# Stores of an intermediate result moved from the ScalarE queue to SP, other stores merged and put off, in a fused FFT filter and two MoE layers on one Trainium2 core

## The chip, the core and the metric

The kernel runs on one core of a Trainium2 chip. That core has a matrix engine (TensorE, "PE"; its weight loads are shown apart as "PEld"), a vector engine (VectorE, "DVE"), ScalarE ("ACT"), GpSimd ("POOL") and SyncE ("SP"), which here does nothing but issue DMAs, in order. ACT and POOL can issue DMAs too. The metric is device time in microseconds; before the change it is 1584.96 us, the median of three runs from 1580.27 to 1590.88 us.

## What is computed

```python
X = np.fft.rfft(x, axis=1)                      # x: 8 x 3072 x 256
Yr = Xr @ w_r - Xi @ w_i + b_r
Yi = Xr @ w_i + Xi @ w_r + b_i
Yr, Yi = softshrink(Yr, 0.01), softshrink(Yi, 0.01)
a = np.fft.irfft(Yr + 1j * Yi, n=3072, axis=1)  # 24576 tokens of 256

h = np.maximum(a @ w_in, 0)                     # 256 -> 2048
y = (s * h * h + b) @ w_out                     # 2048 -> 256

logits = y @ w_gate                             # 8 experts, top 1, 768 places each
out[i] = gate[i] * (relu(y[i] @ w1[e]) @ w2[e]) # only for tokens that got a place
```

Places are given in the order of the tokens, so most of the 24576 tokens get none and their output row is zero.

## The kernel before, in words

**The Fourier filter.** A batch of 3072 rows is transformed in two steps. The first (`f1_mm`, L224) multiplies chunks of x by a 48-point matrix; eight chunks make a batch, and each chunk's result `z` goes to the DRAM tensor `zd`. The second takes the batch in twelve groups, p = 0 to 11, each two frequency rows wide: `g_load` (L264) brings `zp` back from `zd`, `g_a` makes the spectrum (`pf`, `l`), `g_b` and `g_b2` mix it with the weights (`pmx`, `kb`, `t`), `g_soft` shrinks it (`cl`, `t`), `g_c` (L388) does the first step back (`pi`) and copies it to `v`, which goes to the DRAM tensor `vd`. The last step back (`i2_load` L400, `i2_mm` L407, `i2_rows` L428) reads `u` from `vd`, eight pieces i to a batch, writes the transposed activations `ah` on ACT and, for later, `at` with two DVE transposes; `at` goes to the DRAM tensor `ad`.

**The first MoE layer as logits.** For each piece the kernel runs eight units (`s_unit`, L748): four matmuls `ph`, a Relu `r` on ACT and a square `qb` on DVE. A batch is thus 64 units, numbered 0 to 63. Only bounds of the logits are needed for most tokens. Four exact blocks of 256 tokens are computed in full in batch 1 (`x_steps`, L1000: `phx`, `xq`, and a store of `xq` to `sd`), and the few candidates for a place at the end.

**What sets the order.** `run` (L1763) writes the program out by unit: it emits `s_unit`, then the put-off stores in the list `later`, then what the table `plan` holds for this unit, sorted by rank. The plan is made by `plan_batch`: the groups of batch b run during batch b - 1, one group each five units, with steps at the offsets of `GROUP_STEPS` (`g_a` 0, `g_b` 2, `g_b2` 4, `g_soft` 4.1, `g_c` 8) from a start that lies `GROUP_LEAD` = 9 units before that batch's unit 0. A group's `zp` load is emitted six units ahead of its `g_a` (four for p = 0 and 1). `i2_do`, the chunks of the first step and the logits go to the unit in a small window where the sum of planned work is lowest (`best`, L1898). The groups of batch 1 run in batch 0, on a tighter cycle. Within a unit each engine runs in program order.

**DMAs.** All DMAs issued by SP and ACT share eight completion semaphores, shown as DMAHW0 to DMAHW7 in the orders below. They are given out in turn over both engines, and a DMA waits until the last DMA on its semaphore has landed. Before the change `v` is stored by ACT right after its copy (L395, L397); a `z` chunk is stored by SP with four DMAs (L246) one unit after its copy; `at` likewise with four; an `xq` store is emitted right behind its square (L1021). The tiles behind these stores rotate: `v` and `zp` have three buffers, `z` and `xq` share two.

Of the kernel before, what the change touches and what calls it, by code (L numbers as in the profile page):

```python
# [19 lines left out]
C = 256  # L20
# [3 lines left out]
M1 = 48  # L24
# [7 lines left out]
TD = 256  # L32
# [92 lines left out]
S_FROM, S_TO = 19, 62  # L125
LIST_AT = 60
XP = 3
INV_LOAD_AT = 54
FIRST_GROUPS_AT = 26
GROUP_LEAD = 9  # L130
GROUP_CYCLE = 5
GROUP_STEPS = (("g_a", 0), ("g_b", 2), ("g_b2", 4), ("g_soft", 4.1), ("g_c", 8))
FIRST_STEPS = (("g_a", 0.3), ("g_b", 1.3), ("g_b2", 2), ("g_soft", 2.6), ("g_c", 5))
# [17 lines left out]
class Kern:  # L151
# [54 lines left out]
    def f1_load(self, b, c):  # L206

        xv = self.I["x"][b].rearrange("(a n) c -> a n c", n=M2)
        if b == 0 and c % 2 == 1:
            xs = [self.stage()[:, 0:2 * C].rearrange("p (n c) -> p n c", n=2) for k in range(2)]  # L210
            for k in range(2):
                for r in range(2):
                    n2 = 8 * c + 4 * r + 2 * k
                    self.nc.sync.dma_start(out=xs[k][64 * r:64 * r + M1], in_=xv[:, n2:n2 + 2, :])
        else:
            pool, tag = (self.mo, "u") if b == 0 and c > 3 else (self.wk, "x")
            xp = pool.tile([128, 4, C], F32, tag=tag, name="x", bufs=4 if tag == "x" else 3)
            for r in range(2):
                n2 = 8 * c + 4 * r
                self.nc.sync.dma_start(out=xp[64 * r:64 * r + M1], in_=xv[:, n2:n2 + 4, :])  # L220
            xs = [xp[:, 0:2], xp[:, 2:4]]
        self.xt[b, c] = xs

    def f1_mm(self, b, c):  # L224

        nc = self.nc
        xs = self.xt.pop((b, c))
        if b or c % 2 == 1:
            ph = self.hp.tile([128, 2, 512], F32, tag="h", name="pz")
            ps = [ph[:, 0], ph[:, 1]]  # L230
        else:
            ps = [self.psum("pz") for r in range(2)]
        for k in range(2):
            for r in range(2):
                h = slice(64 * r, 64 * r + M1)
                nc.tensor.matmul(ps[r][64 * k:64 * k + 64, :], self.f1[h], xs[k][h].rearrange("p a c -> p (a c)"),  # L236
                                 start=True, stop=True, skip_group_check=True)
        if b:
            zz = self.wk.tile([128, 2, 2, C], F32, tag="z", name="z", bufs=2)
            nc.scalar.copy(out=zz.rearrange("p r a c -> p r (a c)"), in_=ph)  # L240

            def store():
                for r in range(2):
                    for k in range(2):
                        n2 = 8 * c + 4 * r + 2 * k
                        nc.sync.dma_start(out=self.zs[b][n2:n2 + 2].rearrange("n q c -> q n c"), in_=zz[64 * k:64 * k + M1, r])  # L246
            self.later.append(store)
            return
        for r in range(2):
            t = 2 * c + r  # L250
            k = t % 11
            pool, tag, n = ((self.wk, "v", 3), (self.wk, "t", 3), (self.mo, "ah", 2), (self.mo, "asq", 2),
                            (self.wk, "zp", 3))[min(k // 2, 4)]
            z = pool.tile([128, 2, C], F32, tag=tag, name="z", bufs=n)
            if r == 1:
                nc.vector.tensor_copy(out=z.rearrange("p a c -> p (a c)"), in_=ps[r])
            else:
                nc.scalar.copy(out=z.rearrange("p a c -> p (a c)"), in_=ps[r])
            for k in range(2):
                n2 = 8 * c + 4 * r + 2 * k  # L260
                nc.sync.dma_start(out=self.zs[b][n2:n2 + 2].rearrange("n q c -> q n c"), in_=z[64 * k:64 * k + M1])
# [126 lines left out]
    def g_c(self, b, p):  # L388
        nc = self.nc
        t = self.Y.pop((b, p))  # L390
        ps = self.psum("pi1")
        for gi in range(2):
            nc.tensor.matmul(ps[:, gi * C:(gi + 1) * C], self.e[:, 2 * p + gi], t[:, gi * C:(gi + 1) * C], start=True, stop=True)  # L393
        v = self.wk.tile([128, 512], F32, tag="v", name="v", bufs=3)
        nc.scalar.copy(out=v, in_=ps)  # L395
        dst = self.vd[b].rearrange("n (r g) c -> (n r) (g c)", r=4)
        nc.scalar.dma_start(out=dst[:, 2 * p * C:(2 * p + 2) * C], in_=v)  # L397


    def i2_load(self, b, i):  # L400
# [49 lines left out]
    def f1_items(self, b):  # L450
        it = []
        for k in range(8):
            def f(k=k):
                self.f1_mm(b, k)
                if b:
                    self.x_ahead(8 * b + k + (XP if b < 3 else XP - 1))
            it.append(f)
        return it

    def x_ahead(self, n):  # L460

        while self.xn <= min(n, 8 * self.B - 1):
            self.f1_load(*divmod(self.xn, 8))
            self.xn += 1
# [535 lines left out]
    def x_steps(self, dtile, lgpool, ga, out, m0, hidden, rows, ptile, keep=None, yout=None):  # L1000

        nc = self.nc
        x = {}
        qs, ys = {}, {}

        def a():
            x["a"] = self.x_in(dtile(), ga(), ptile)
            x["lg"] = lgpool()
            if yout is not None:
                x["y"] = ptile("ya").rearrange("p (m c) -> p m c", m=2)  # L1010

        def mm(v):
            ps = hidden()
            self.x_mm(ps, x["a"], v)
            q = qs[v] = rows()
            nc.scalar.activation(out=q, in_=ps, func=AF.Relu)
            nc.vector.tensor_tensor(out=q, in0=q, in1=q, op=ALU.mult)
            if yout is not None:
                ys[v] = self.x_out(x["y"], q, v)
            if keep is not None:  # L1020
                nc.sync.dma_start(out=keep[2 * v:2 * v + 2, :, 128 * m0:128 * m0 + TD].rearrange("f p n -> p f n"), in_=q)  # L1021

        def lg(v):
            for k in (v, v + 1):
                self.x_lg(x["lg"], qs, k)
            if yout is not None:
                for k in (v, v + 1):
                    ys.pop(k)()

        def end():  # L1030
            ls = self.rp.tile([128, TD], F32, tag="ls", name="ls2", bufs=1)
            nc.scalar.copy(out=ls, in_=x["lg"][:, :TD])
            x["ls"] = ls
            if yout is not None:
                y = self.pb.tile([128, 2, C], F32, tag="y", name="y", bufs=1)
                nc.vector.scalar_tensor_tensor(out=y, in0=x["y"], scalar=self.ws, in1=self.yb.unsqueeze(1).to_broadcast([128, 2, C]),
                                               op0=ALU.mult, op1=ALU.add)
                nc.sync.dma_start(out=yout.rearrange("(m p) c -> p m c", p=128), in_=y)

        def fin():  # L1040
            pt = ptile("plt")
            for m in range(2):
                nc.tensor.transpose(pt[:, m * 128:(m + 1) * 128], x["ls"][:, m * 128:(m + 1) * 128], self.ident)
            nc.vector.tensor_reduce(
                out=out[:, m0:m0 + 2], in_=pt[:, :TD].rearrange("p (m j e) -> p m e j", m=2, j=4)[:, :, 0:E],
                axis=AX.X, op=ALU.add)
        it = [a]
        for v in range(8):
            it.append(lambda v=v: mm(v))
            if v % 2 == 0 and v > 1:  # L1050
                it.append(lambda v=v: lg(v - 2))
        return it + [lambda: lg(6), end, fin]
# [710 lines left out]
    def run(self):  # L1763
        tc, nc, B = self.tc, self.nc, self.B
# [5 lines left out]
        with ExitStack() as es, tc.manual_schedule():  # L1770
# [225 lines left out]
            for b in range(B):  # L1996
                if b == B - 1:
                    e2.close()
                    p2 = es.enter_context(tc.tile_pool(name="p2", bufs=1, side="right", reuse_waits="tile"))
                    e4 = es.enter_context(ExitStack())  # L2000
                    self.p2c = e4.enter_context(tc.tile_pool(name="p2c", bufs=1, side="right", reuse_waits="tile"))
                    self.yf = [p2.tile([128, C], F32, tag=f"yf{j}", name=f"yf{j}") for j in range(NJ)]
                if b:
                    plan_batch(b)
                for k in range(64):
                    i, u = divmod(k, 8)
                    self.s_unit(b, i, u)
                    while self.later:
                        self.later.pop(0)()
                    for e in sorted(plan.pop(64 * b + k, []), key=lambda e: e[:3]):  # L2010
                        e[3]()
                    assert b < B - 1 or k < LIST_AT or not todo
                    if todo:
                        todo.pop(0)()
                    if u == 7:
                        del self.aT[b, i]
# [29 lines left out]
```

## Time and profile before

| | us |
|---|---|
| median of 3 runs (lowest to highest) | 1584.96 (1580.27 to 1590.88) |
| the profiled execution: its own time | 1582.95 |
| its span, first to last instruction | 1580.9 |
| PE busy in it | 1402.5 (89%) |
| DVE, ACT, POOL busy | 961.3 (61%), 800.7 (51%), 268.6 (17%) |
| DMA moved | 230.40 MB, 146 GB/s mean |

The page of the profile gives shares over the whole span. Since the kernel has stages (batch 0 with its conversions to about 330 us, batch 1 with the exact blocks to about 545, five even batches to about 1250, batch 7 and the tail), the questions here need the answers by stage and the time line: there a row gives start, duration, engine, line, and in brackets how long the engine sat idle before it and what released it. The granted clock is a share of full speed, and it has two levels, 1.2 and 2.4 GHz, so 0.74 over a stretch means that 52% of it ran at the lower one.

### The profile page before, as it was taken

What the parts mean: (1) busy time and instruction counts of PE and PEld (TensorE: products, weight loads), DVE (VectorE), ACT (ScalarE), POOL (GpSimd) and SP (SyncE); (2) the same over time, 40 slices, a digit from 0 to 9 for tenths busy, and PEclk for the clock granted to TensorE, in tenths of its full rate; (3) what the DMA queues carried; (4) which work ended last, traced back from release to release, by engine and by line L of the source; (5) the groups of instructions that cost most, each with busy time, mean ns of one, the idle gap of its engine ahead of it and who ended that gap; (6) DMA issues with size and microseconds to landing.
All of it is one profiled execution on the core that took longest, in us unless ns stands there. A gap on an engine that the chain in (4) does not pass through costs nothing. (4 is left out here: it accounts for less than half of the span.)

```text
span 1580.9 us, 32575 instructions
## 1 busy us (share of the span) xinstructions
PE 1402.5 (89%) x12797; PEld 1153.8 (73%) x12797; DVE 961.3 (61%) x2078; ACT 800.7 (51%) x1132; POOL 268.6 (17%) x235
## 2 busy tenths in 40 slices
PE   6995859989999988999999999999999868999984
PEld 3975637778788766777777877777888747988872
DVE  1775426765655877667677756776687675653410
ACT  1334533455555655665665655565656555652311
POOL 0444110000000013002010200110030171223020
PEclk8897879999999989999999989999999988999997
DMA  8726685645655545655755755565445456630052
GB/s 201 243 90 189 159 209 145 182 127 155 182 162 154 136 113 154 163 148 125 190 141 148 170 140 152 134 180 140 135 108 136 104 142 174 161 107 18 15 196 100
DMA packets 271370, 230.40 MB, mean 146 GB/s; under 512 B 123582, under 2 KB 231872, under 8 KB 271201
## 3 DMA queue, kind: packets, MB, share of 16 engines
q1 hardware_dynamic: 253408, 200.13, 47.9%
q10 hardware_dynamic: 13968, 25.20, 4.4%
q0 software_dynamic: 3824, 2.82, 0.7%
q8 instruction: 105, 1.72, 0.4%
q14 instruction: 65, 0.52, 0.1%
HBM read 114.17 MB, written 114.09 MB: 144 GB/s over the span
## 5 line engine op out<-in xcount | busy, mean ns | idle before, releaser
L762 ACT ACTIVATE r<-ph 128x768 bf16<-128x768 f32 (+1 forms) x512 | 399.6, 784 | 283.7 <-PE ph L757 250.6
L757 PE MATMUL ph<-ah,win 128*128 128x384 f32 (+1 forms) x2048 | 498.4, 369 | 36.4 <-ACT r L762 20.1
L763 DVE TENSOR_TENSOR qb<-r 128x768 bf16<-128x768 bf16 (+1 forms) x512 | 299.8, 587 | 269.3 <-ACT r L762 266.0
L757 PEld LDWEIGHTS ph<-ah,win 128*128 128x128 f32 x2048 | 350.8, 197 | 130.5 <-ACT r L762 54.2
L355 PE MATMUL pmx<-wm,l 128*128 128x256 f32 x1196 | 302.6, 392 | 8.0 <-DVE l L317 2.8
L425 POOL TENSOR_TENSOR asq<-ah 128x768 bf16<-128x768 f32 x64 | 95.9, 1498 | 969.3 <-ACT ah L422 953.7
L355 PEld LDWEIGHTS pmx<-wm,l 128*128 128x128 f32 x1196 | 229.7, 197 | 40.0 <-DVE l L317 3.6
L278 PE MATMUL pf<-d,zp 128*128 128x128 f32 x672 | 93.3, 283 | 23.8 <-DMA zp<-zd 23.8
L278 PEld LDWEIGHTS pf<-d,zp 128*128 128x128 f32 x672 | 89.2, 198 | 27.4 <-DMA zp<-zd 26.4
L393 PE MATMUL pi<-t,e 128*128 128x256 f32 x384 | 99.4, 382 | 1.0 <-DVE t L378 0.6
L236 PE MATMUL pz<-x,f 48*64 48x512 f32 x480 | 78.4, 697 | 14.6 <-DVE at L434 9.5
L419 PEld LDWEIGHTS pi<-f1t,u 48*64 48x64 f32 x4096 | 68.7, 136 | 29.1 <-issue 11.9
L419 PE MATMUL pi<-f1t,u 48*64 48x48 f32 x4096 | 76.7, 224 | 11.5 <-ACT z L240 6.8
L434 DVE STREAM_TRANSPOSE at<-pi 128x384 f32<-128x384 f32 x128 | 66.9, 560 | 26.9 <-ACT ah L422 22.3
L240 ACT COPY z<-pz 128x1024 f32<-128x1024 f32 x56 | 56.7, 1013 | 50.9 <-PE pz L236 30.5
L911 POOL DMA_INDIRECT list<-c,x x64 | 64.8, 1012 | 82.6 <-DVE c L907 66.7
L393 PEld LDWEIGHTS pi<-t,e 128*128 128x128 f32 x384 | 71.5, 191 | 7.6 <-PE ph L757 1.1
L350 DVE TENSOR_TENSOR t<-t,cl 128x512 f32<-128x512 f32 x96 | 74.6, 777 | 3.3
L422 ACT CAST ah<-pi 128x768 fp32r<-128x768 f32 x64 | 51.2, 801 | 49.1 <-PE pi L419 49.1
L395 ACT COPY v<-pi 128x512 f32<-128x512 f32 x96 | 56.3, 587 | 38.2 <-PE pi L393 33.2
L281 ACT COPY l<-pf 128x512 f32<-128x512 f32 x84 | 49.3, 587 | 51.6 <-PE pf L278 47.4
L793 ACT COPY ls<-lg 128x384 f32<-128x384 f32 (+1 forms) x64 | 53.6, 837 | 19.4 <-PE lg L780 15.2
(408 smaller groups left out, 1815.5 us busy)
## 6 DMA issues: line engine op xcount, KB each, us to landing
zd<-z SPq DMA_DIRECT2D x256, 96.0 KB
zp<-zd SPq DMA_DIRECT2D x96, 256.0 KB
vd<-v ACTq DMA_DIRECT2D x96, 256.0 KB
u<-vd SPq DMA_DIRECT2D x128, 192.0 KB
ad<-at SPq DMA_DIRECT2D x256, 96.0 KB
out<-zero SPq DMA_DIRECT2D x96, 256.0 KB
x<-x SPq DMA_DIRECT2D x120, 192.0 KB
sd<-xq SPq DMA_DIRECT2D x32, 256.0 KB
```

The source lines that it names most:

```text
L236: nc.tensor.matmul(ps[r][64 * k:64 * k + 64, :], self.f1[h], xs[k][h].rearrange("p a c -> p (a c)"), start=True, stop=True, skip_group_che ...
L278: nc.tensor.matmul(pv[:, h, :, gi * 64:gi * 64 + 64], zp[:, gi, h * 128:(h + 1) * 128], self.d[:, 2 * p + gi, :].rearrange("p (t m) -> p t ...
L350: nc.vector.tensor_tensor(out=t, in0=t, in1=cl, op=ALU.subtract)
L355: self.nc.tensor.matmul(o, part(h), w[:, h], start=start and h == 0, stop=stop and h == 1, skip_group_check=True)
L393: nc.tensor.matmul(ps[:, gi * C:(gi + 1) * C], self.e[:, 2 * p + gi], t[:, gi * C:(gi + 1) * C], start=True, stop=True)
L419: nc.tensor.matmul(o[64 * k:64 * k + 64, :, n], u[p, n, 128 * k + h:128 * k + 128:2], self.f1t[p], start=True, stop=True, skip_group_check ...
L425: nc.gpsimd.tensor_tensor(out=self.asq[b, i], in0=af, in1=af, op=ALU.mult)
L434: nc.vector.transpose(out=at[:, :, :, h], in_=pv[:, M1 * h:M1 * (h + 1)])
L757: nc.tensor.matmul(ps[:, j, :n], self.win[:, k, f], ah[:, k, t0:], start=(k == 0), stop=(k == 1))
L762: nc.scalar.activation(out=r, in_=ps[:, :, :n], func=AF.Relu)
L763: nc.vector.tensor_tensor(out=q, in0=r, in1=r, op=ALU.mult)
L911: self.nc.gpsimd.indirect_dma_start(out=self.lists[n], out_offset=bass.IndirectOffsetOnAxis(ap=x[:, n:n + 1], axis=0), in_=c[:, n:n + 1], ...
```

## The change

Seven edits, all of them in what is issued where and when:

- `v` stores of batches 1 to 7 go to the list `later` and are issued by SP, behind the next unit's `s_unit`; those of batch 0 stay on ACT.
- A `z` chunk of batches 1 to 7 is stored with two DMAs of 192 KB instead of four of 96 KB.
- To make that possible, the rows of x in a chunk are taken in another arrangement. The two loads of a chunk stay two, as pieces of 2 KB instead of 4 KB.
- `xq` stores of the exact blocks go to `later` and are issued at the next step's start or the next unit.
- The list is emptied by a function `flush`, called by the loop over units as before and at the start of each exact step.
- `GROUP_LEAD` goes from 9 to 10: all groups of batches 2 to 7 run one unit earlier. What `best` places moves with it.
- `INV_LOAD_AT` goes from 54 to 55: the first two `u` loads of the next batch are emitted one unit later.

```diff
-INV_LOAD_AT = 54
+INV_LOAD_AT = 55
-GROUP_LEAD = 9
+GROUP_LEAD = 10
...
-                n2 = 8 * c + 4 * r
-                self.nc.sync.dma_start(out=xp[64 * r:64 * r + M1], in_=xv[:, n2:n2 + 4, :])
+                n2 = 8 * c + (2 if b else 4) * r
+                src = xv[:, n2:n2 + 4, :] if not b else xv[:, 8 * c:8 * c + 8, :].rearrange("a (k r n) c -> a r k n c", k=2, r=2)[:, r]
+                self.nc.sync.dma_start(out=xp[64 * r:64 * r + M1] if not b else xp[64 * r:64 * r + M1].rearrange("p (k n) c -> p k n c", k=2), in_=src)
...
             def store():
-                for r in range(2):
-                    for k in range(2):
-                        n2 = 8 * c + 4 * r + 2 * k
-                        nc.sync.dma_start(out=self.zs[b][n2:n2 + 2].rearrange("n q c -> q n c"), in_=zz[64 * k:64 * k + M1, r])
+                for k in range(2):
+                    n2 = 8 * c + 4 * k
+                    nc.sync.dma_start(out=self.zs[b][n2:n2 + 4].rearrange("n q c -> q n c"),
+                                      in_=zz[64 * k:64 * k + M1].rearrange("p r a c -> p (r a) c"))
...
-        nc.scalar.dma_start(out=dst[:, 2 * p * C:(2 * p + 2) * C], in_=v)
+
+        def store():
+            (nc.sync if b else nc.scalar).dma_start(out=dst[:, 2 * p * C:(2 * p + 2) * C], in_=v)
+        if b:
+            self.later.append(store)
+        else:
+            store()
...
+    def flush(self):
+        while self.later:
+            self.later.pop(0)()
...
         def mm(v):
+            self.flush()
...
             if keep is not None:
-                nc.sync.dma_start(out=keep[2 * v:2 * v + 2, :, 128 * m0:128 * m0 + TD].rearrange("f p n -> p f n"), in_=q)
+                self.later.append(lambda: nc.sync.dma_start(
+                    out=keep[2 * v:2 * v + 2, :, 128 * m0:128 * m0 + TD].rearrange("f p n -> p f n"), in_=q))
...
-                    while self.later:
-                        self.later.pop(0)()
+                    self.flush()
```

Two places show what this does to the order. The first is SP's queue in the middle of an even batch (batch 4 before, batch 3 after; the loads of x, a chunk's stores and a `zp` load, with the semaphores that each waits for). Before:

```order
L403 DMA u<-vd_88 48x4x256 [waits DMAHW5_49,PE_49]
L403 DMA u<-vd_88 48x4x256 [waits DMAHW7_49]
L220 DMA x<-x 48x1024 [waits DMAHW0_49,PE_49]
L220 DMA x<-x 48x1024 [waits DMAHW1_49]
L246 DMA zd<-z 48x2x256 [waits DMAHW2_49,Activation_49]
L246 DMA zd<-z 48x2x256 [waits DMAHW3_49]
L246 DMA zd<-z 48x2x256 [waits DMAHW4_49]
L246 DMA zd<-z 48x2x256 [waits DMAHW5_49]
L267 DMA zp<-zd 128x512 [waits DMAHW6_49,PE_49]
```

DMAHW6 is skipped between the two `u` loads: a `v` store of ACT has it there. Now:

```order
L221 DMA x<-x 48x2x512 [waits DMAHW5_49]
L221 DMA x<-x 48x2x512 [waits DMAHW6_49]
L400 DMA vd_88<-v 128x512 [waits DMAHW7_49,Activation_49]
L246 DMA zd<-z 48x4x256 [waits DMAHW0_49,Activation_49]
L246 DMA zd<-z 48x4x256 [waits DMAHW1_49]
L268 DMA zp<-zd 128x512 [waits DMAHW2_49,PE_49]
```

The `v` store has come into SP's queue and waits for ACT's copy itself; the chunk's stores are two; the `zp` load waits for a semaphore of SP's own eight DMAs back.

The second is DVE in batch 4, at the transposes of its piece i = 1 (`at`). Before, they stand behind a group's `g_b2` and `g_soft` (the rows `t` and `cl`) with no unit in between:

```order
L763 TENSOR_TENSOR qb<-r 128x768
L375 TENSOR_TENSOR t<-pmx,kb 64x256
L376 TENSOR_TENSOR t<-pmx,kb 64x256
L377 TENSOR_TENSOR t<-pmx,bias_154 64x256
L378 TENSOR_TENSOR t<-pmx,bias_154 64x256
L349 TENSOR_SCALAR cl<-t 128x512
L350 TENSOR_TENSOR t<-t,cl 128x512
L434 STREAM_TRANSPOSE at<-pi_9411 128x384 x2
```

Now the six rows of the group lie two units (two `qb`) ahead of the transposes:

```order
L379 TENSOR_TENSOR t<-pmx,bias_154 64x256
L350 TENSOR_SCALAR cl<-t 128x512
L351 TENSOR_TENSOR t<-t,cl 128x512
L880 TENSOR_TENSOR LG<-LG,cd 96x256
L774 TENSOR_TENSOR qb<-r 128x768
L283 TENSOR_TENSOR l<-pf_9329,l 128x2x128
L885 TENSOR_REDUCE mu<-LG 96x32
L774 TENSOR_TENSOR qb<-r 128x768
L441 STREAM_TRANSPOSE at<-pi_9350 128x384 x2
```

The group runs a unit earlier and the piece stayed, so its transposes no longer queue behind the group's six operations. Over batches 2 to 6 the pieces whose transposes stand right behind `g_soft` go from 15 (i = 1, 4 and 6 of each) to 10 (i = 2 and 4 of each).

## Rows read from the trace of the kernel before

**Rows 1.** The page: the span, and busy us (share) and instructions by engine.

```profile
span 1580.9 us, 32575 instructions
PE 1402.5 (89%) x12797; PEld 1153.8 (73%) x12797; DVE 961.3 (61%) x2078; ACT 800.7 (51%) x1132; POOL 268.6 (17%) x235
```

**Rows 2.** Windows by stage: length, busy by engine (instructions), granted clock, DMA share, GB/s.

```profile
330.00:545.00 215.00, 206.19 (x1977) 170.26 (x1974) 134.50 (x294) 115.64 (x163) 13.62 (x10) 0.99 0.54 154
545.00:690.00 145.00, 128.32 (x1176) 102.87 (x1175) 104.29 (x258) 81.19 (x108) 26.25 (x23) 0.92 0.54 142
```

**Rows 3.** Waits of PE, whole span: us in total, times, longest.

```profile
PE pf L278 <- DMA zp<-zd: 23.8, 7, 7.1
...
PE ph L757 <- DVE at L434: 13.6, 9, 1.8
```

**Rows 4.** Waits of SP's queue, whole span.

```profile
SPq L1978 <- DMA vd<-v: 59.9, 13, 7.0
...
SPq L1021 <- DVE xq L1017: 50.4, 27, 4.5
...
SPq L267 <- DMA vd<-v: 33.3, 5, 10.5
```

**Rows 5.** Time line: PE's `zp` stalls, with SP's load and ACT's store before one.

```profile
630.54 2.08 PE L278 MATMUL pf<-d,zp 128*128 128x128 f32 x8 [6.89 <-DMA zp<-zd]
775.72 2.08 PE L278 MATMUL pf<-d,zp 128*128 128x128 f32 x8 [2.45 <-DMA zp<-zd]
913.11 0.33 ACTq L397 DMA_DIRECT2D vd<-v  x1
917.20 0.36 SPq L267 DMA_DIRECT2D zp<-zd  x1
920.09 2.08 PE L278 MATMUL pf<-d,zp 128*128 128x128 f32 x8 [3.62 <-DMA zp<-zd]
1064.60 0.60 PE L278 MATMUL pf<-d,zp 128*128 128x128 f32 x3 [1.83 <-DMA zp<-zd]
```

**Rows 6.** Windows around stalls; the granted clock is the third value from the end.

```profile
560.00:580.00 20.00, 14.46 (x80) 10.70 (x79) 15.90 (x46) 9.39 (x15) 1.47 (x1) 0.74 0.33 84
620.00:640.00 20.00, 13.11 (x121) 9.74 (x123) 8.71 (x17) 6.61 (x10) 7.46 (x8) 0.74 0.53 140
765.00:785.00 20.00, 17.55 (x160) 14.18 (x158) 12.47 (x23) 10.04 (x14) 1.47 (x1) 0.91 0.63 169
915.00:935.00 20.00, 16.38 (x118) 12.45 (x111) 8.79 (x17) 8.07 (x11) 1.47 (x1) 0.74 0.55 141
1060.00:1080.00 20.00, 18.17 (x158) 13.82 (x156) 10.70 (x21) 10.01 (x13) 1.47 (x1) 0.83 0.65 170
205.00:240.00 35.00, 20.31 (x166) 13.91 (x166) 8.38 (x32) 10.22 (x15) 1.73 (x2) 0.71 0.79 208
```

**Rows 7.** Time line of PE: waits for the transposes; the largest, and first and last.

```profile
567.57 1.99 PE L236 MATMUL pz<-x,f 48*64 48x512 f32 x8 [4.06 <-DVE at L434]
669.56 1.50 PE L757 MATMUL ph<-ah,win 128*128 128x384 f32 x4 [1.83 <-DVE at L434]
1235.01 0.96 PE L757 MATMUL ph<-ah,win 128*128 128x384 f32 x4 [1.83 <-DVE at L434]
```

**Rows 8.** Time line in batch 0: a chunk's copy on ACT, and PE's two stalls.

```profile
213.09 1.01 ACT L240 COPY z<-pz 128x1024 f32<-128x1024 f32 x1 [7.23 <-DMA zd<-z]
214.16 1.96 PE L419 MATMUL pi<-f1t,u 48*64 48x48 f32 x64 [6.80 <-ACT z L240]
231.88 2.07 PE L278 MATMUL pf<-d,zp 128*128 128x128 f32 x8 [7.14 <-DMA zp<-zd]
```

**Rows 9.** One line's issues: duration in ns (min/median/max), first and last start in us.

```profile
L397 ACTq DMA_DIRECT2D vd<-v x96: 325/326/365, 61.4 to 1250.4; - x96
L246 SPq DMA_DIRECT2D zd<-z x224: 315/430/1087, 172.6 to 1099.4; - x112
```

## The prediction

> **What bounds the kernel now.** I read the page first: PE is busy for 1402.5 of 1580.9 us, no other engine (its own weight loads apart) for more than 61% [rows 1]. So the kernel is as long as PE's work plus its holes. The windows by stage say where the holes are: batch 1 with the exact blocks leaves PE idle for 8.8 of 215 us at full clock, the stage behind it, batch 2, for 16.7 of 145 us at a clock of 0.92 [rows 2]. The list of PE's waits names the causes that a change of stores can reach: 23.8 us for `zp` loads in seven waits, and 13.6 us for DVE's transposes at one line alone [rows 3]. The list of SP's waits then shows why a `zp` load can be late: SP stood for `v` stores for 59.9 us at the stores of zeros and for 33.3 us, in only five waits, at `zp` loads [rows 4]. A `zp` load does not read `vd`; all that ties it to a `v` store is the shared completion semaphore. The time line shows one case whole [rows 5]: ACT issues its `v` store at 913.11, SP's `zp` load goes out at 917.20, and PE, which had stood 3.62 us for it, starts at 920.09. The other three such stalls in even batches are of 6.89, 2.45 and 1.83 us [rows 5].
>
> A stall costs more than its length. Behind the one at 630.54 the clock is 0.74 over 20 us, so 10.4 us ran at 1.2 GHz, the lower level [rows 6]; the `pf` matmuls just behind three of the stalls take 2.08 us [rows 5]. A Relu unit's `ph` shows the same: 1.50 us behind a stall, 0.96 us where the clock had not fallen [rows 7].
>
> **The change, part by part.**
>
> *A, the shared semaphores.* ACT's 84 `v` stores of batches 1 to 7 leave the ring of semaphores, and a `zp` load of SP can then wait only for SP's own DMAs. The new wait is the store's own: it stands right ahead of a `zp` load in SP's queue and waits for ACT's copy. That copy belongs to the unit before, the load is needed six units later, so I let this cost nothing; the cover is those six units, and if it is gone the load is as late as now (the first rival). Gain: the four stalls sum to 14.8 us. Each lies at a piece i = 4, where the transposes still stand behind `g_soft`; there the wait for DVE, 1.83 us as in [rows 7], comes to the surface when the load is on time. So 14.8 - 4 x 1.83 = 7.5 us. The clock: the windows at 0.74, 0.91, 0.74 and 0.83 hold 10.4 + 3.6 + 10.4 + 6.8 = 31.2 us at the lower level [rows 6]. If all the stalled time lay in them, 16.4 us of work ran at half rate and cost 8.2 us; if none did, 15.6 us. I take 8, near the lower end, since the DVE stalls that stay cost some clock too. **A = 16 us**, between 0 (the loads stay late) and 30.
>
> *B, the groups one unit earlier.* In the order of DVE the pieces whose transposes stand right behind a group's `g_b2` and `g_soft` go from 15 to 10 in batches 2 to 6. The trace has eleven PE waits for the transposes there, the largest of 4.06 us and ten of 1.75 to 1.83 us, from 669.56 to 1235.01 [rows 7]; the other four pieces are those under A. The 4.06 us one, at i = 1 of batch 2, where a chain of bounds is in the way as well, loses the group, and so does one more piece in each even batch: 4.06 + 4 x 1.83 = 11.4 us. The clock of the first is 0.74, 10.4 us at the lower level, less at most 4.1 us of stall, half of the rest: 3.2 us [rows 6]. For the other four I take 0.9 us each, half of what a full 3.6 us at the lower level would cost (the window at 765 has 0.91 [rows 6]), as the first stall of [rows 7] slowed what followed and the last did not: 3.6 us. **B = 18 us**, between 0 (other pieces take their place) and 24.
>
> *C, fewer `z` stores in batch 0.* While the chunks of batch 1 are made, PE works 20.3 of 35 us at a clock of 0.71 with the DMA engines 79% busy [rows 6]. ACT stands 7.23 us at a chunk's copy because the chunk two before is not stored, and PE 6.80 us behind it; then PE stands 7.14 us for the first `zp` [rows 8]. Two issues less for each chunk save SP 2 x 0.43 = 0.86 us [rows 9], some 5 us over the six chunks before that load, and four waits for a semaphore become two. The bytes stay, and the engines are 79% busy, so the transfers do not get faster by as much. **C = 5 us**, between 0 and 14 (both stalls gone).
>
> *D, what I cost at nothing.* SP issues 112 DMAs less (2 x 56 chunks) and 84 more; at 0.43 us each that frees 12 us of a queue that has many waits. ACT loses 84 x 0.33 = 28 us of issuing [rows 9], hidden since it is busy 51% of the time [rows 1]; without that cover the gain would be up to 28 us more. The loads of x are not fewer: the order shows two to a chunk before and now, with smaller pieces, and none of the stalls in [rows 5, 7, 8] is for x. The `u` loads a unit later follow a group that ends a unit earlier, which is also why they still stand behind the last `v` store by one unit, on the same wait.
>
> *E, the exact blocks' stores put off.* SP stood 50.4 us, 27 times, at these stores for DVE [rows 4], so SP was there 1.9 us too early on average, and putting them off first uses up that time. But `xq` and `z` share two buffers; if a store goes out later than before, ACT waits for the buffer. Batch 1 has next to no holes to hide that in [rows 2]. Bounds: 0, and 32 x 1.9 = 60 us if each of the 32 stores were later by what SP used to wait. It is nearest to 0; I take **4 us lost**.
>
> *Against the sum.* The Trainium skill (DMA: Bandwidth & Descriptors, "Issuing engines are not separate DMA queues") says that DMAs of all issuing engines run on the same 16 DMA engines, and that issuing from several only saves sequencer time. By that rule alone the move from ACT to SP gives nothing and adds 84 issues to SP: A would be 0. The rows under A differ: what goes is not a transfer's time but a wait of SP for a store that another engine had yet to issue. The rule's outcome is the first rival below, with its price from rows.
>
> **Sum.** 16 + 18 + 5 - 4 = 35 us. The profiled execution's own time is 1582.95 us, which gives 1548; the median of the runs is 2.0 us above that execution, so I predict **1550 us**.
>
> **The rivals.**
> 1. *SP only changes what it waits for.* The `v` store in SP's queue waits for ACT, ACT for PE, and the `zp` load behind it is late as before. For it: SP issues in order, and it ran behind by units at 913 to 917 [rows 5]. Against it: the copy is six units older than the need. A falls away: 1585 - 18 - 5 + 4 = 1566 us. Chance 0.17.
> 2. *The transposes' wait moves.* Other pieces, or other operations in the units that `best` now chooses, hold DVE up as often as before. For it: the new order has pieces with a logit reduction ahead of the transposes. Against it: those are short, and the count of full blocks falls. B falls away: 1585 - 16 - 5 + 4 = 1568 us. Chance 0.13.
> 3. *Both*: only C and E are left, 1584 us, no change. Chance 0.10.
> 4. *Slower: buffers of the exact blocks.* A put-off `xq` store lands later, the two shared buffers come free later, and ACT, in order, holds Relu and with it PE, in the one stage that has no holes. At the upper price of 60 us under E: 1585 - 39 + 60 = 1606 us. It decides from 39 / 32 = 1.2 us per store on (no gain left), and the kernel is slower by over 1% from 1.7 us per store. For it: the stage is full. Against it: PE loses only 8.8 us there now, so the buffers have some slack. Chance 0.10.
>
> The forecast has what is left, 0.50, and its own range is 1530 to 1566 us (A and B near their upper bounds; or either half as large).
>
> **How the numbers follow.** Within 1% means 1569 to 1601 us, about what a measurement of this kernel can tell from no change. Faster: the forecast whole (0.50) and about two thirds of rivals 1 and 2, whose prices lie just under that line (0.18): 0.68. Same: the rest of them and rival 3: 0.21. Slower: rival 4, and a little for a wait that I do not see: 0.11. The range that leaves out 1 in 10 at either end reaches from the forecast's lower end to rival 3: 1530 to 1587 us.
>
> **What would show it.** After the change, A is right if SP has no long wait for `vd<-v` at `zp` loads, and PE's waits for `zp` in batches 2 to 5 fall from 14.8 us to under 3; wrong if SP now waits as long for ACT's `v` at L400. B is right if PE's waits for the transposes there go from fifteen places to ten, with none of 4 us; wrong if the transposes' wait is as large in sum. C is right if the stalls at 214 and 232 us shrink by some 5 us together. E shows as waits of ACT at `xq` or `z` for stores to `sd`, and as PE losing more than 13 us of batch 1. The clock of the stage behind the exact blocks should rise above 0.92 [rows 2]. What would make the prediction wrong is a wait that stands nowhere in this trace: the put-off stores and the `v` stores in one queue have not been seen together.

## The result, and the profile after

The changed kernel takes 1547.28 us, the median of four runs from 1546.11 to 1548.25; the kernel before took 1584.39 us beside it (four runs, 1580.27 to 1590.88). The ratio is 0.9762, with a 95% interval from 0.9728 to 0.9796: 37 us gained. The profiled execution took 1547.21 us, with a span of 1545.2.

The page of the changed kernel has the same 12797 matmuls as [rows 1], and PE busy for 8 us less with them:

```profile
span 1545.2 us, 32455 instructions
PE 1394.6 (90%) x12797; PEld 1153.3 (75%) x12797; DVE 954.9 (62%) x2078; ACT 801.1 (52%) x1132; POOL 266.0 (17%) x235
```

PE's busy time fell by 7.9 us and its idle time by 27.8 us. The windows that answer to [rows 2], with the columns as there, say in which stage:

```profile
330.00:545.00 215.00, 207.15 (x1994) 171.51 (x1988) 136.82 (x299) 117.46 (x166) 13.48 (x10) 1.00 0.56 157
545.00:690.00 145.00, 134.46 (x1289) 109.33 (x1286) 109.14 (x267) 86.22 (x114) 27.17 (x24) 0.96 0.59 148
```

Batch 1 changed little (PE idle for 7.9 us where it was 8.8). In batch 2 PE gained 6.1 us of work in the same 145 us, and the granted clock went from 0.92 to 0.96.

The waits of PE from 545 to 1125 us, which is batches 2 to 5 and a part of 6 (us in total, times, longest), have no `zp` load worth the name any more. In the kernel before the same stretch has 15.3 us of it in five waits, 14.8 of them the four stalls of [rows 5]:

```profile
PE pz L237 <- DVE at L441: 12.6, 7, 1.8
PE pnr L735 <- DVE nrm L728: 5.2, 1, 5.2
...
PE pf L279 <- DMA zp<-zd: 0.2, 1, 0.2
```

SP's queue tells why. Its waits over the whole span, to be read beside [rows 4]:

```profile
SPq L400 <- ACT v L396: 147.5, 51, 7.1
...
SPq L1033 <- DVE xq L1029: 47.9, 29, 5.1
SPq L410 <- DMA vd<-v: 41.1, 8, 29.2
```

The 33.3 us that SP stood for `vd<-v` at `zp` loads are gone. In their place SP stands 51 times, 147.5 us in all, for ACT's copy at the `v` store itself. The time line of SP in batch 4 shows what this does to the load behind it:

```profile
881.52 0.34 SPq L400 DMA_DIRECT2D vd<-v  x1
881.95 0.38 SPq L268 DMA_DIRECT2D zp<-zd  x1
...
891.68 0.35 SPq L400 DMA_DIRECT2D vd<-v  x1
892.13 0.38 SPq L268 DMA_DIRECT2D zp<-zd  x1
```

Each `zp` load goes out 0.4 us behind a `v` store, and 10.2 us behind the load before it, an even pace. From 545 to 1125 us none is late for PE by more than 0.2 us: the six units between load and use cover the wait for ACT.

The transposes' waits are seen in PE's time line; the first row is the place of the 4.06 us wait of [rows 7], the others are two of the waits of batches 2 to 6 and the last of them:

```profile
561.42 0.59 PE L735 MATMUL pnr<-nrm,ones 128*128 128x4 f32 x2 [5.22 <-DVE nrm L728]
...
587.60 1.09 PE L237 MATMUL pz<-x,f 48*64 48x512 f32 x8 [1.84 <-DVE at L441]
...
898.73 1.09 PE L237 MATMUL pz<-x,f 48*64 48x512 f32 x8 [1.84 <-DVE at L441]
...
1169.76 0.45 PE L768 MATMUL ph<-ah,win 128*128 128x384 f32 x1 [1.83 <-DVE at L441]
```

Nine such waits stand in batches 2 to 6, at 1.61 to 1.84 us, where the new order leaves ten pieces behind a group; the tenth (batch 3, i = 2) shows none. What differs there is what GpSimd does meanwhile. The time lines of DVE and GpSimd show `cl`, one of the group's six operations, at the tenth place and at the wait of 898.73:

```profile
722.95 0.43 DVE L350 TENSOR_SCALAR cl<-t 128x512 f32<-128x512 f32 x1
724.29 1.47 POOL L432 TENSOR_TENSOR asq<-ah 128x768 bf16<-128x768 f32 x1 [7.39 <-ACT ah L429]
...
895.14 1.47 POOL L432 TENSOR_TENSOR asq<-ah 128x768 bf16<-128x768 f32 x1 [16.01 <-ACT ah L429]
895.40 1.49 DVE L350 TENSOR_SCALAR cl<-t 128x512 f32<-128x512 f32 x1
```

Where the piece's `asq` runs on GpSimd at the same time, `cl` takes 1.49 us. From 545 to 1250 us that is so at nine groups, the nine waits; at the other 49 `cl` takes 0.50 us or less. By these rows 1.06 us of a wait of 1.83 us is not the queue of six operations but one of them that takes longer beside GpSimd. No run here moves the one without the other, so how much of a wait would stay with `asq` elsewhere is not shown.

The hole at 4.06 us did not go: the transposes left it and the bounds' chain (`nrm`) fills it with 5.22 us, where before PE had waited 1.20 us for that chain and then the 4.06.

In batch 0 the two stalls of [rows 8] are a little shorter, 5.61 for 6.80 us and 6.56 for 7.14, and the window over them has the clock of [rows 6], 0.71:

```profile
212.73 1.96 PE L426 MATMUL pi<-f1t,u 48*64 48x48 f32 x64 [5.61 <-ACT z L241]
230.01 2.07 PE L279 MATMUL pf<-d,zp 128*128 128x128 f32 x8 [6.56 <-DMA zp<-zd]
```

To see where the time went in each kernel I took the start of PE's first `pi` matmul of the last step back (`i2_mm`) of batches 1, 2 and 7 from the time lines. Lengths in us of one execution each:

| kernel | batch 0 | batch 1 | batches 2 to 6 | batch 7 and tail |
|---|---|---|---|---|
| before | 337.2 | 202.5 | 717.1 | 324.1 |
| the change | 333.2 | 201.6 | 686.9 | 323.5 |
| e1_lead | 334.9 | 211.1 | 707.9 | 324.3 |
| e2_vsp | 337.6 | 201.2 | 703.2 | 324.1 |
| e3_zx | 332.4 | 204.0 | 701.0 | 319.8 |
| e4_exact | 336.5 | 204.2 | 717.0 | 320.7 |
| e5_noB | 339.3 | 201.2 | 699.3 | 320.7 |
| e6_noA | 333.5 | 212.9 | 698.4 | 323.8 |
| e7_gb2 | 332.4 | 200.0 | 667.8 | 318.9 |
| e8_vpool | 334.9 | 201.3 | 687.2 | 318.7 |
| e9_gb2_old | 337.4 | 207.4 | 708.7 | 321.1 |
| e10_vpool_gb2 | 333.1 | 199.9 | 668.2 | 320.3 |

The last column scatters by 5.6 us without a pattern in the edits (e4_exact has the orders of before there), so a difference of that size in one column of one execution decides nothing. With a lead of 10 (the change, e1_lead, e6_noA, e7_gb2, e8_vpool, e10_vpool_gb2) `best` places the first piece of batches 1 and 2 one unit earlier than with 9, so against the other kernels these columns read some 2 us too short for batch 0 and as much too long for batches 2 to 6. Counted to the same unit instead (the first Relu `r` of a batch), the change's gain of 35.7 us lies in batches 2 to 6 (31.6; 30.2 by the table) and batch 0 (3.1; 4.0 by the table).

### The profile page after: what moved, and what is told of

Read it like the earlier page. It is cut to its first block, busy times and chain, and to the rows that moved or that the text cites. A ratio compares the mean times of both kernels' runs of the same rounds, so it can differ in the third digit from the quotient of the medians.

```text
span 1545.2 us, 32455 instructions
## 1 busy us (share of the span) xinstructions
PE 1394.6 (90%) x12797; PEld 1153.3 (75%) x12797; DVE 954.9 (62%) x2078; ACT 801.1 (52%) x1132; POOL 266.0 (17%) x235
## 5 line engine op out<-in xcount | busy, mean ns | idle before, releaser
L356 PE MATMUL pmx<-wm,l 128*128 128x256 f32 x1196 | 299.4, 390 | 7.1 <-DVE l L318 2.8
L279 PE MATMUL pf<-d,zp 128*128 128x128 f32 x672 | 90.0, 277 | 7.0 <-DMA zp<-zd 6.8
```

What stands on the lines that cost most here:

```text
L279: nc.tensor.matmul(pv[:, h, :, gi * 64:gi * 64 + 64], zp[:, gi, h * 128:(h + 1) * 128], self.d[:, 2 * p + gi, :].rearrange("p (t m) -> p t ...
L356: self.nc.tensor.matmul(o, part(h), w[:, h], start=start and h == 0, stop=stop and h == 1, skip_group_check=True)
```

## The experiments

Each kernel was timed against the kernel before on the same chip; the ratios carry the verdicts, the medians are for reading. The theory was the prediction's: A (the `v` stores leave the shared semaphores), B (the groups a unit earlier) and C (fewer `z` stores) give 16, 18 and 5 us, each by itself, and E (the exact blocks' stores put off) costs 4. The first four kernels put one part alone into the kernel before, the next two take one out of the change.

**e1_lead: B alone.**

```diff
-INV_LOAD_AT = 54
+INV_LOAD_AT = 55
-GROUP_LEAD = 9
+GROUP_LEAD = 10
```

> The kernel before with GROUP_LEAD 10 and INV_LOAD_AT 55 alone; v stores stay on ACT, z stores stay four. Theory (the terms add up: B is the transposes behind g_soft, A the shared semaphores): 1566 us, 18 less than before; the pieces whose transposes wait go from 15 to 10, and PE's waits for zp in batches 2 to 5 stay near 14.8 us, perhaps at other groups. Rival (the zp waits go because the groups run earlier, not because of the semaphores): 1552 us, and PE's zp waits there under 3 us. Rival (other pieces take over): 1584 us.

Measured: 1577.55 us beside 1580.98, ratio 0.9975 (0.9949 to 1.0). B alone gives about 4 us (0 to 8), not 18. The five pieces did leave the groups, and the waits that stay are ten of the old size. But the `zp` stalls, which had lain at pieces i = 4, now stand by themselves, at 10.8 us in sum, and batch 1 is 8.6 us longer, where PE now waits for the exact blocks' loads (`ga`). Both are in PE's time line of this kernel, the `ga` wait first:

```profile
354.44 0.67 PE L963 MATMUL pt<-ident,ga 128*128 128x128 f32 x2 [4.76 <-DMA ga<-ad]
...
658.61 1.16 PE L278 MATMUL pf<-d,zp 128*128 128x128 f32 x8 [1.83 <-DMA zp<-zd]
...
799.93 1.56 PE L278 MATMUL pf<-d,zp 128*128 128x128 f32 x8 [2.75 <-DMA zp<-zd]
...
942.86 1.16 PE L278 MATMUL pf<-d,zp 128*128 128x128 f32 x8 [2.75 <-DMA zp<-zd]
...
1086.51 1.43 PE L278 MATMUL pf<-d,zp 128*128 128x128 f32 x8 [3.44 <-DMA zp<-zd]
```

Of the four `zp` loads behind these stalls only the first waits for a `v` store itself (4.5 us). The other three go out right behind a `u` load that stood 7.1 to 8.2 us for one, as SP's time line shows ahead of the stall at 799.93:

```profile
788.44 8.19 SPq L403 DMA_DIRECT2D u<-vd  x2
796.72 0.39 SPq L267 DMA_DIRECT2D zp<-zd  x1
```

**e2_vsp: A alone.**

```diff
-INV_LOAD_AT = 54
+INV_LOAD_AT = 55
...
-        nc.scalar.dma_start(out=dst[:, 2 * p * C:(2 * p + 2) * C], in_=v)
+
+        def store():
+            (nc.sync if b else nc.scalar).dma_start(out=dst[:, 2 * p * C:(2 * p + 2) * C], in_=v)
+        if b:
+            self.later.append(store)
+        else:
+            store()
```

> The kernel before with the v stores of batches 1 to 7 on SP, one unit later, and INV_LOAD_AT 55 (so that the loads still follow the last store); lead 9, z stores four. Theory: 1568 us, 16 less; no zp waits of PE in batches 2 to 5, still 15 pieces with the transposes behind g_soft, now fifteen waits of 1.8 us with one of 4. Rival (which queue issues a store only matters for the time to issue it): 1584 us, PE's zp waits as before, and SP waiting for ACT's v in place of the v stores.

Measured: 1566.36 us, ratio 0.9903 (0.9869 to 0.9938), 15 us faster. As the theory had it: no `zp` stall in batches 2 to 5, and the transposes' waits are all there. From 545 to 1125 us PE's waits begin:

```profile
PE pz L236 <- DVE at L440: 15.0, 7, 4.0
PE ph L763 <- DVE at L440: 7.3, 4, 1.8
```

**e3_zx: C alone** (with the x rows that it needs).

```diff
-                n2 = 8 * c + 4 * r
-                self.nc.sync.dma_start(out=xp[64 * r:64 * r + M1], in_=xv[:, n2:n2 + 4, :])
+                n2 = 8 * c + (2 if b else 4) * r
...
-                for r in range(2):
-                    for k in range(2):
-                        n2 = 8 * c + 4 * r + 2 * k
-                        nc.sync.dma_start(out=self.zs[b][n2:n2 + 2].rearrange("n q c -> q n c"), in_=zz[64 * k:64 * k + M1, r])
+                for k in range(2):
+                    n2 = 8 * c + 4 * k
+                    nc.sync.dma_start(out=self.zs[b][n2:n2 + 4].rearrange("n q c -> q n c"),
+                                      in_=zz[64 * k:64 * k + M1].rearrange("p r a c -> p (r a) c"))
```

> The kernel before with the z stores in two issues instead of four and the loads of x in the other arrangement, nothing else. Theory: 1580 us, 4 less, all of it in batch 0 (the change gained 4.0 us up to the first piece of batch 1); zp waits in batches 2 to 5 as before. Rival (fewer DMAs on the shared semaphores let zp loads past the v stores too): 1570 us, with the zp waits there smaller. Rival (the pieces of 2 KB slow the loads of x): 1590 us.

Measured: 1562.4 us, ratio 0.9894 (0.987 to 0.9917). My theory missed by 18 us and the rival held: the gain is as large as that of e2_vsp and lies in the same place, 16.1 of it in batches 2 to 6, though `v` is still stored by ACT. PE's `zp` waits from 545 to 1125 us have shrunk to almost nothing, while SP (second fence, the same stretch) still stands for `v` stores:

```profile
PE pf L279 <- DMA zp<-zd: 1.2, 2, 0.8
```

```profile
SPq L1979 <- DMA vd<-v: 46.6, 9, 6.7
SPq L404 <- DMA vd<-v: 40.3, 10, 5.7
SPq L221 <- DMA vd<-v: 35.0, 11, 5.8
SPq L268 <- DMA vd<-v: 31.8, 6, 9.5
```

The last line is the `zp` load: in the kernel before it stands 31.4 us in this stretch (four waits, the longest 10.5), so this waiting did not go either. What changed is which load it falls on. Before, it is the load of the ninth group (p = 8), which goes out 2.9 to 3.7 us ahead of its use in the four stalls. In e3_zx the longest wait of each batch falls on the load of the tenth group, which goes out 10.4 to 13.5 us ahead; ACT's store, SP's load and PE's use in one case, to be read beside 913.11, 917.20 and 920.09 of [rows 5]:

```profile
902.91 0.33 ACTq L398 DMA_DIRECT2D vd<-v  x1
...
906.39 0.37 SPq L268 DMA_DIRECT2D zp<-zd  x1
...
918.44 1.05 PE L279 MATMUL pf<-d,zp 128*128 128x128 f32 x8
```

With two DMAs less to each chunk, the semaphore that a late `v` store holds comes round at another DMA of SP, and SP reaches the load with time to spare. It is the place in the ring that cost the 15 us, not the waiting as such: at the four lines SP stands 154 us for `v` stores, and PE waits 1.2 us.

**e4_exact: E alone.**

```diff
+    def flush(self):
+        while self.later:
+            self.later.pop(0)()
...
+            self.flush()
...
-                nc.sync.dma_start(out=keep[2 * v:2 * v + 2, :, 128 * m0:128 * m0 + TD].rearrange("f p n -> p f n"), in_=q)
+                self.later.append(lambda: nc.sync.dma_start(
+                    out=keep[2 * v:2 * v + 2, :, 128 * m0:128 * m0 + TD].rearrange("f p n -> p f n"), in_=q))
```

> The kernel before with the stores of xq put off to the next step or unit, nothing else. Theory: 1584 us, within 2 us of before, as the changed kernel's batch 1 took 0.9 us less than before. Rival (E as predicted, hidden in the changed kernel by gains elsewhere in batch 1): 1588 us, ACT waiting for sd<-xq.

Measured: 1581.38 us, ratio 1.0002 (0.9979 to 1.0024). Neither a loss nor a gain beyond 4 us.

**e5_noB: the change without B.**

```diff
-GROUP_LEAD = 10
+GROUP_LEAD = 9
```

> The changed kernel with GROUP_LEAD back at 9: v stores on SP, z stores in two, xq put off. Theory (v on SP and two z stores remove the same zp waits, so their gains do not add; the lead's gain shows only once those waits are gone): 1563 us, no zp waits of PE in batches 2 to 5, fifteen pieces with transposes behind g_soft. Rival (the gains add as measured alone, 15 + 18, and the lead is worth 3): 1551 us.

Measured: 1563.67 us beside 1582.36, ratio 0.9885 (0.982 to 0.9951). A, C and E together give 18 us, no more than A alone or C alone: both remove the same four stalls. The transposes' waits are back, 24.2 us of them from 545 to 1125 us for the change's 12.6:

```profile
PE pz L237 <- DVE at L441: 16.9, 8, 4.0
PE ph L768 <- DVE at L441: 7.3, 4, 1.8
```

**e6_noA: the change without A.**

```diff
-
-        def store():
-            (nc.sync if b else nc.scalar).dma_start(out=dst[:, 2 * p * C:(2 * p + 2) * C], in_=v)
-        if b:
-            self.later.append(store)
-        else:
-            store()
+        nc.scalar.dma_start(out=dst[:, 2 * p * C:(2 * p + 2) * C], in_=v)
```

> The changed kernel with the v stores back on ACT right behind their copy; z stores in two, xq put off, lead 10. Theory (what matters is whether a zp load has the same completion semaphore as a v store that ACT issues later; by the order no zp load of batches 2 to 5 has in this kernel): 1549 us, PE's zp waits there under 1 us. Rival (SP's queue must be rid of ACT's stores, wherever they fall): 1562 us, zp waits of 8 us or more.

Measured: 1563.9 us, ratio 0.9876 (0.9813 to 0.9939). The time is that of the rival, 1562, but not by its reason: `zp` does not stall in batches 2 to 5, as the theory said. By the table the loss against the change is 11.3 us in batch 1, as in e1_lead, and 11.5 in batches 2 to 6; by the medians it is 16.6 in all. The profiled execution, 1570.77 us, is 7 us above its median, so the lengths in the table are rather high for this kernel. In batches 2 to 6 PE's longer waits are nearly those of the change and the granted clock is a little lower (0.93 for 0.96 from 560 to 700 us, 0.98 for 0.99 from 700 to 1120), so whether the edit costs anything there stays open. In batch 1 the stall's whole chain stands in the time lines of PE, SP and ACT:

```profile
353.07 0.67 PE L968 MATMUL pt<-ident,ga 128*128 128x128 f32 x2 [4.69 <-DMA ga<-ad]
...
343.23 8.21 SPq L1867 DMA_DIRECT2D ga<-ad  x8
...
348.76 0.33 ACTq L398 DMA_DIRECT2D vd<-v  x1
```

SP stands 5.6 us for `v` stores here, in two waits: 3.1 us ahead of the first of eight `ga` issues, and the rest ahead of the eighth, so that these issues take 8.21 us. ACT issues the second of the stores that fall here at 348.76. The changed kernel has the same piece of program without that:

```profile
340.57 5.78 SPq L1873 DMA_DIRECT2D ga<-ad  x8
...
348.14 0.48 PE L974 MATMUL pt<-ident,ga 128*128 128x128 f32 x2 [0.17 <-DMA ga<-ad]
```

So with the lead of 10 the exact blocks' `ga` loads are the ones that meet the late stores, and A is needed for them.

**e7_gb2: the waits that B left.** In batches 2 to 6 the planner puts two pieces of each batch behind a group since it counts `g_b2` at 0.86. At 2.0 it puts none there in batches 1 to 6.

```diff
-WORK = {"g_a": 0.87, "g_b": 1.72, "g_b2": 0.86, "g_soft": 0.0, "g_c": 0.86}
+WORK = {"g_a": 0.87, "g_b": 1.72, "g_b2": 2.0, "g_soft": 0.0, "g_c": 0.86}
```

> The changed kernel with the planned work of g_b2 set from 0.86 to 2.0, which makes the planner put no piece's transposes behind g_b2 and g_soft (none of batches 1 to 6, ten in the changed kernel). Theory B: ten waits of 1.8 us and some clock go: 1525 us, PE's waits for the transposes under 4 us. Rival (DVE is late in these batches anyway and another operation takes the place): 1545 us.

Measured: **1521.14 us** (1520.38 to 1522.32), ratio 0.9609 (0.9548 to 0.9671). It beats both kernels, the change by 26 us. PE has no wait for the transposes of 0.9 us or more between 300 and 1180 us, and the list for 545 to 1125 us now begins with the bounds' chain. The second fence is the window from 700 to 1120 us of this kernel, the third that of the changed one:

```profile
PE pnr L735 <- DVE nrm L728: 5.2, 1, 5.2
PE ph L768 <- ACT r L773: 2.6, 5, 1.9
```

```profile
700.00:1120.00 420.00, 415.61 (x4072) 340.36 (x4070) 310.40 (x655) 270.14 (x350) 66.34 (x57) 1.00 0.62 161
```

```profile
700.00:1120.00 420.00, 408.94 (x4006) 332.89 (x3999) 299.22 (x628) 264.31 (x342) 60.05 (x49) 0.99 0.62 158
```

PE is idle for 4.4 us of 420 where the change leaves 11.1, and the clock shows 1.00. Of the 26.1 us between the two spans 19.1 are in batches 2 to 6; the change's nine waits there sum to 16.3. The move takes the groups' `cl` out of reach of GpSimd's `asq` as well (0.61 us at most from 545 to 1250 us), so the gain is that of both.

**e8_vpool: another queue for A.** The `v` stores go to GpSimd, right behind the copy; in the order its DMAs have semaphores of their own (DMASW).

```diff
-
-        def store():
-            (nc.sync if b else nc.scalar).dma_start(out=dst[:, 2 * p * C:(2 * p + 2) * C], in_=v)
-        if b:
-            self.later.append(store)
-        else:
-            store()
+        (nc.gpsimd if b else nc.scalar).dma_start(out=dst[:, 2 * p * C:(2 * p + 2) * C], in_=v)
```

> The changed kernel with the v stores of batches 1 to 7 issued by GpSimd right behind the copy, on its own completion semaphores. Theory (the stores only have to leave the semaphores that SP shares): 1547 us, as the changed kernel. Rival (the queue of GpSimd is in the way: asq waits behind the store's wait for ACT and its descriptors): 1560 us, DVE or PE waiting for POOL.

Measured: 1542.29 us, ratio 0.9738 (0.9676 to 0.98). As the theory said, it is enough that the stores leave the semaphores of SP's loads; neither SP nor the later issue matters. SP waits for `v` stores at the `u` loads alone (35.5 us), as in the change. GpSimd stands for ACT's copy, as this row of its time line shows, but from 330 to 1220 us PE never waits for GpSimd:

```profile
884.37 0.59 POOL L398 DMA_DIRECT2D vd<-v  x1 [2.65 <-ACT v L396]
```

The 5 us by which its median lies under the change's are not shown as a gain: the intervals overlap, and in the table they lie in batch 7 and the tail, almost all of it after the last `v` store.

**e9_gb2_old: the same planner's number in the kernel before.**

```diff
-WORK = {"g_a": 0.87, "g_b": 1.72, "g_b2": 0.86, "g_soft": 0.0, "g_c": 0.86}
+WORK = {"g_a": 0.87, "g_b": 1.72, "g_b2": 2.0, "g_soft": 0.0, "g_c": 0.86}
```

> The kernel before with one number changed: the planned cost of g_b2 from 0.86 to 2.0, so that no piece's transposes stand right behind a group in batches 2 to 6. The v stores stay on ACT, and the order still gives zp loads of batches 2 to 5 a semaphore of a later v store. Theory (the pieces' waits and the zp stalls cover each other, both have to go): PE has no wait of 0.9 us or more for the transposes there, but zp stalls of 2 to 5 us stay in at least three of the four batches, about 12 us with their clock; about 1565 us. Rival (the 26 us that this number gave in the changed kernel come whatever the stores do, five more pieces even): 1582 - 26 = 1556 us or less, down to 1545.

Measured: 1577.0 us beside 1594.33 on this chip, ratio 0.9885 (0.9857 to 0.9913): 18 us (14 to 23), the theory's 17 and not the rival's 26 or more. All the waits for the transposes are away, and the `zp` stalls stay in all four batches; a chunk's copy on ACT is late once, too:

```profile
639.75 2.07 PE L278 MATMUL pf<-d,zp 128*128 128x128 f32 x8 [4.96 <-DMA zp<-zd]
...
779.31 0.92 PE L278 MATMUL pf<-d,zp 128*128 128x128 f32 x5 [1.64 <-DMA zp<-zd]
...
890.56 1.65 PE L757 MATMUL ph<-ah,win 128*128 128x384 f32 x4 [6.73 <-ACT z L240]
...
928.90 1.16 PE L278 MATMUL pf<-d,zp 128*128 128x128 f32 x8 [2.94 <-DMA zp<-zd]
...
1069.56 1.16 PE L278 MATMUL pf<-d,zp 128*128 128x128 f32 x8 [1.31 <-DMA zp<-zd]
```

**e10_vpool_gb2: both that beat the change.** The edits of e7_gb2 and e8_vpool together:

```diff
-WORK = {"g_a": 0.87, "g_b": 1.72, "g_b2": 0.86, "g_soft": 0.0, "g_c": 0.86}
+WORK = {"g_a": 0.87, "g_b": 1.72, "g_b2": 2.0, "g_soft": 0.0, "g_c": 0.86}
...
+        (nc.gpsimd if b else nc.scalar).dma_start(out=dst[:, 2 * p * C:(2 * p + 2) * C], in_=v)
```

> The changed kernel with both edits that beat it: v stores on GpSimd right behind the copy, and the planned cost of g_b2 at 2.0. Theory (the two touch different engines and different waits): the gains add, 1547 - 26 - 5 = 1516 us. Rival (the 5 us of GpSimd's stores lay in the stretches around the pieces that no longer wait): 1521 us, as with the planned cost alone.

Measured: 1522.36 us, ratio 0.9556 (0.9495 to 0.9618), on a chip where before took 1594.33. The median is the rival's 1521; by the ratio alone, against e7_gb2's 0.9609, a gain of some 5 us is not excluded. The spans, 1521.5 and 1519.1 us, show none.

## Why the prediction held, step by step

The time came out 3 us under the forecast, and the sum of A and B, 34 us, is near the 31.6 us that batches 2 to 6 gave. But the steps are not the independent terms as which they were added, and that the total fits so closely is in part luck. Of B, the 7.3 us priced at the 4.06 us wait did not come, and other places gave more than their price. The larger worth of C, 12 us beyond its price, is hidden in the whole change by A.

- **A, 16 us: right in size and mechanism.** Alone it gives 15 us (e2_vsp). The stalls for `zp` went from 15.3 to 0.2 us, and the cover of six units held although SP now stands 147.5 us for ACT's copies. Where the prediction fell short is in what A is: not a matter of SP, since GpSimd does as well (e8_vpool), nor of the `v` stores alone, since fewer `z` stores move the same stalls away (e3_zx). Nor must it be the load's own semaphore, as the prediction has it: in e1_lead three of four late loads are held by the DMA ahead of them.
- **B, 18 us: right beside A, wrong alone.** From e5_noB to the change the medians differ by 16.4 us; by the ratios, each with its own kernel before, it is 19 us, give or take 12. Counted to the same unit, 13.6 us of it lie in batches 2 to 6. Alone B gives 4 us. Two steps failed here. The larger is that the new lead puts the `ga` loads of batch 1 in the way of late `v` stores (batch 1 is 8.6 us longer in e1_lead, 11.3 in e6_noA), a price that the prediction did not have because it looked for shared semaphores at `zp` loads only. The other is that the pieces' waits and the `zp` stalls were priced as two lists. They share their places: a `zp` stall at a piece i = 4 hides the transposes' wait there, which the prediction did subtract under A; what it missed is the same thing from the other side, that moving the groups leaves the `zp` stall standing alone. In batches 3 to 5, counted to the same unit, B gives 3.6 us alone and 10.1 beside A, in one execution each. One place of B was wrong within it: at the 4.06 us wait another chain of DVE ends 5.22 us late. And the prediction took a wait for the six operations' queue alone; 1.06 us of it is `cl` beside GpSimd.
- **C, 5 us: the mechanism half right.** Counted to the same unit, batch 0 became 3.1 us shorter in the change, with its two stalls 1.8 shorter in sum; alone C gives 4.8 there (e3_zx). The larger effect of this edit, 16 us in batches 2 to 6, the prediction put at nothing: of SP's queue it counted the time of the issues saved and not that the ring of semaphores turns with every DMA left out. In the whole change this does not show, since A removes the same stalls.
- **D, nothing: not contradicted.** SP's 84 more and 112 fewer issues leave no trace among PE's waits.
- **E, 4 us lost: not seen** (e4_exact lies between 3.3 us gained and 3.8 lost). PE loses 7.9 us of batch 1 and not over 13, and SP stands 47.9 us at these stores for 50.4: putting them off did not even use up SP's waiting.
- **The rivals.** Rivals 1 and 2 as such did not come: SP's new wait is long but falls on nothing, and the transposes' waits fell as the order said. Yet their prices, 1566 and 1568 us for the change with one half gone, are near what e6_noA and e5_noB measure, 1563.9 and 1563.7; for e6_noA that is luck, since no `zp` stall came back and the `ga` loads paid instead. Rival 4 is refuted by e4_exact.
- **The skill's rule.** In e2_vsp and e8_vpool the same 84 stores of 256 KB go out from another engine, and the kernel gets 15 us faster or stays as fast as with SP. The Trainium skill (DMA: Bandwidth & Descriptors, "Issuing engines are not separate DMA queues") allows for a change of issuing engine only the sequencer's time. These runs differ from it: which engine issues decides also whose semaphores a store holds, and so which load waits behind it.

What stays open: how the 16 us of B beside A divide between the waits and the clock, how a transposes' wait divides between the queue and GpSimd, and why batch 0 takes 339.3 us in e5_noB, with A and C, where A alone has 337.6 and C alone 332.4.

## What to carry to other kernels

Where DMAs of several engines share a rotating set of completion semaphores, look up which late store each urgent load, and each DMA ahead of it in its queue, has to wait for, and do so again after any edit that adds or drops a DMA: here dropping 112 unrelated stores was worth as much as moving the guilty ones. Two stalls that fall on the same place are not two gains; take the one out, look at what the other then does, and add up only what was measured together. And where an order is planned, charge a step the time of the engine on which it blocks others: one planned cost, raised from 0.86 to 2.0, gave 26 us more, and `g_b2` with `g_soft` behind it keeps DVE busy for 2.8 us (the six operations at 721 us of the changed kernel), 1.06 us more beside GpSimd.

## What the runs showed of the hardware

The same DVE operation, `cl` on 128 x 512 values, takes 0.43 to 0.50 us alone and 1.49 us while GpSimd's `asq` runs: 49 and 9 times from 545 to 1250 us of the changed kernel. In the kernel before it is 45 times 0.43 to 0.54 us alone, and 13 times 1.48 or 1.49 us of the 14 that overlap an `asq`.

A short stall does not always cost clock. The changed kernel's window around the 1.84 us wait at 898.73 has a granted clock of 1.00, and so all of it at 2.4 GHz; the one around the 1.83 us wait at 1036.49, of the same length and with as much work of PE, has 0.91, so 3.6 us of 20 at the lower level of 1.2 GHz:

```profile
890.00:910.00 20.00, 18.16 (x215) 14.81 (x217) 12.58 (x24) 11.97 (x16) 1.47 (x1) 1.00 0.57 160
...
1030.00:1050.00 20.00, 18.16 (x223) 14.66 (x222) 12.02 (x23) 10.88 (x14) 1.47 (x1) 0.91 0.57 158
```

Over the even batches the sum is small: 0.96 from 700 to 1120 us before, 0.99 after, 1.00 with e7_gb2. No run here shows what decides between the two.
